# Gated mix of linear attention and a squared-ReLU network on one core: key sums through GpSimd, split piece transfers, low halves on VectorE, a fold by banks

## The chip, the core and the metric

The kernel runs on one core of a Trainium2 chip. Its time is the device time of one execution in microseconds (us); the kernel before the change takes 513.42 us (median of three runs, 512.58 to 514.22). A core has five engines, each with its own instruction queue that is worked off strictly in order: TensorE (PE, matrix products into the accumulation memory PSUM), VectorE (DVE), ScalarE (ACT), GpSimd (POOL) and SyncE (SP, which here only issues transfers). Transfers between memory and the on-chip SBUF, and inside SBUF, are issued by SP, ACT or GpSimd and carried by 16 DMA engines.

## The reference

```python
x = A_x                                     # 1 x 2048 x 512
g = sigmoid((x * gate_w).sum(-1))
qkv = x @ wqkv                              # 32 heads of 16
phi = lambda z: concat(softmax(z @ w_phi), softmax(-(z @ w_phi)))   # 32 features a head
kv  = einsum("sf,sd->fd", phi(k), v)        # per head
z   = phi(k).sum(over s)                    # per head: the key sums
o   = (phi(q) @ kv) / (phi(q) @ z + 1e-6)
a   = o @ wo
b   = relu(x @ w1 + b1) ** 2 @ w2 + b2      # 1792 hidden units
out = g * a + (1 - g) * b                   # everything in float32
```

## The kernel before

Every float32 product that matters is made of three faster ones: each operand is split into a high half (rounded, `hi`) and a low half (`src - hi`), and TensorE adds high x high, high x low and low x high (`mm3`, L76 to L78). ScalarE makes the high half, VectorE the low half (`split`, L61), except where the code names another engine.

The 2048 rows are worked in 4 blocks of 512, each block in 4 chunks of 128. There are two sweeps over the blocks. Sweep 1 runs the first 7 of the 14 hidden tiles of the network; between them it builds keys, values and the products phi(k)^T v, collected in the PSUM tile `kvps`. Sweep 2 runs the other 7 hidden tiles; between them it makes the queries, their features, numerators and the output projection. In both, `u` is the first network product (x times w1), `hh` and `hl` are the halves of its squared ReLU, `d` is the second (times w2). A table of slots (`at`) says after which `u` or `d` each other step is written; the order in which an engine then gets its instructions is made by a scheduler from that program, from priorities (`tc.high_priority`) and from pinned successions (`tc.issue_after`). So PE's order is: half a `u`, something of the attention, the other half, four chunks of `d`, and so on.

What happens between the sweeps and at the head of sweep 2, in the order of the work:

- `query_fold` (L192) multiplies w_phi into the query weights: 16 small matmuls on 32 x 32 corners of PE, row group r and column group g, bank r of four PSUM banks. ScalarE copies the banks out (`cp`), VectorE turns them, transfers lay them out (`wq`).
- `kv_most` and `kv_done` (L783, L791) bring `kvps` out in two parts. `kv_done` copies four groups of 17 rows (`kvt`), adds them to the first part on GpSimd (L796, four instructions), stores the key sums into `zrow` (L797) and spreads each half of `zrow` over all 128 partitions (L800, `vext`). Both kinds of transfer are issued by SP.
- For each query chunk n, `q_exps` (L362) takes maximum and minimum of the projected query tile `q`, subtracts, exponentiates on ScalarE (L343, tile `e`), and multiplies by the spread key sums on GpSimd (L368, `ez`, two instructions). `q_phi` (L371) reduces (`sm` L325, `dz` L378), works out the denominator in small steps (`r`, `dz`, `den`, `w`, L327 and L379 to L386) and scales `e` (L348).
- `transposed` (L392) turns 32 x 32 blocks on VectorE (`tb`, L394) and moves 12 pieces of 32 x 256 into `phiT` by transfers on SP's queue (L403); the four pieces on the diagonal are ScalarE copies (`diagonal`, L409).
- Two chunks make a pair. `numer` (L415) multiplies both chunks' `phiT` by the key-value blocks on PE (`num`, L420) and splits the result into `o`; ScalarE makes the high halves, VectorE the low ones. `attended` (L441) then multiplies `o` by the output weights (`att`). `phiT` and `o` have a single buffer, `tb` has two.

Two loads of x for the next block go by `do_x` (L627) and `load_x` (L110): in the block after the first of sweep 2 the low halves `xl` are GpSimd's, pinned behind the first `ez`; in the later blocks they are VectorE's.

Of the kernel before, what the change touches and what calls it, by code (L numbers as in the profile page):

```python
# [34 lines left out]
def tile_gated_mix(ctx: ExitStack, tc: tile.TileContext, xT, xn, wqT, wkT, wphi, wv, wo, w1, b1, w2, b2, gw, out):  # L35
# [25 lines left out]
    def split(src, hi, lo, ehi, elo):  # L61
        if ehi is nc.scalar:
            i = nc.scalar.activation(hi, src, AF.Copy)  # L63
        else:
            i = ehi.tensor_copy(hi, src)
        st["lo"] = elo.tensor_tensor(lo, src, hi.bitcast(F32), ALU.subtract)  # L66
        return i
# [39 lines left out]
        st["ffn"] = split(t, hi, lo, nc.scalar, nc.vector)  # L107
        return hi, lo

    def load_x(b, after=None):  # L110
        xs = []
        for k in range(NK):
            t = load(xT[b, :, k, :])
            hi = xpool.tile([P, SB], F32R, tag="xh", name=f"xh{b}_{k}")
            lo = xpool.tile([P, SB], F32R, tag="xl", name=f"xl{b}_{k}")
            with tc.issue_after(after.ins) if after else nullcontext():
                split(t, hi, lo, nc.scalar, nc.gpsimd if after else nc.vector)
            xs.append((hi, lo))
        return xs

# [71 lines left out]
    def query_fold():  # L192
        pss = [bank(f"fold{r}") for r in range(4)]
        wph, *t = st["wT"]
        for g in range(NK):
            for r in range(4):
                rows, cols = slice(32 * r, 32 * r + 32), slice(32 * g, 32 * g + 32)
                with tc.issue_after(st["up"].ins):
                    st["up"] = nc.tensor.matmul(
                        pss[r][cols, :], wph[rows, g * P + 32 * r:g * P + 32 * r + 32],  # L200
                        t[g][rows, :].rearrange("p (k c q) -> p c k q", c=4, q=32),
                        start=True, stop=True, skip_group_check=True)
        piece = lambda u, nm: work.tile([P, 2 * D], F32, tag=f"o{u}", name=nm, bufs=1)
        part_ = lambda t: t.rearrange("p (c k r q) -> p c k r q", c=2, k=NK, q=32)
        cps = [piece(u, "cp") for u in range(2)]
        for u, cp in enumerate(cps):
            for r in range(4):
                with tc.high_priority(offset=AHEAD):
                    nc.scalar.activation(
                        part_(cp)[:, :, :, r, :],  # L210
                        pss[r][:, 256 * u:256 * u + 256].rearrange("p (c k q) -> p c k q", c=2, q=32), AF.Copy)
        tbs = [work.tile([P, 2 * D], F32, tag="tb", name="turned", bufs=2) for _ in range(2)]
        for cp, tb in zip(cps, tbs):
            with tc.high_priority(offset=AHEAD):
                nc.vector.transpose(tb, cp)
        st["wq"] = [piece(u, "wq") for u in range(2)]
        for u, w in enumerate(st["wq"]):
            for c in range(4):
                for g in range(2):
                    (nc.sync, nc.gpsimd)[c % 2].dma_start(  # L220
                        w[32 * c:32 * c + 32, 512 * g:512 * g + 512],
                        tbs[c // 2][32 * (2 * u + g):32 * (2 * u + g) + 32, 512 * (c % 2):512 * (c % 2) + 512])
# [166 lines left out]

    def transposed(phi, pt, u):  # L392
        tb = work.tile([P, 2 * D], F32, tag="tb", name="tb", bufs=2)
        st["tb"] = nc.vector.transpose(tb, phi)  # L394
        later = []
        for j in range(4):
            for r in range(4):
                dst = pt[32 * j:32 * j + 32, u, r, :, :].rearrange("p g s -> p (g s)")
                src = tb[32 * r:32 * r + 32, 256 * j:256 * j + 256]
                if j == r:  # L400
                    later.append((dst, src))
                else:
                    st["pieces"] = nc.sync.dma_start(dst, src)  # L403
        return later

    def diagonal(n):
# [219 lines left out]

    def do_x(b):  # L627
        with tc.issue_after(st["act"].ins), tc.issue_after(st["pieces0" if b == NB + 2 else "act"].ins):
            st["x", b] = load_x(b % NB, st["ez"] if b == NB + 1 else None)

    ROWS = [divmod(o, 2) for o in (2, 3, 4, 5, 6, 7, 0, 1)]
    LASTP = len(ROWS) - 1
# [59 lines left out]
    def pair_steps(p, s):  # L692
# [19 lines left out]
        def run(i):  # L712
            first, other = i in (1, 2, 7), "Y" if i in (2, 7, 4) else "X"
            if i == 1:
                if p == 0:
                    banks.remove(ps_e)
                v["X"] = ps_e.tile([P, 512], F32, tag="s", name="pX")
            elif first:
                v["bank"] = banks[0]
                v["Y"] = bank("pY")  # L720
            elif i == 4:
                used(v["bank"])
            block(v[other], p, i, first)
            with tc.high_priority(offset=AHEAD), again(p, i, 0):
                if i in (1, 6, 5):
                    v[i] = st["tmp"][0][:, 512 * (i == 6):512 * (i == 6) + 512]
                    read = nc.scalar.activation(v[i], v["X"], AF.Copy)  # L727
                elif i == 7:
                    return
                else:  # L730
                    t, half, u = {2: (n, 0, 1), 3: (n, 1, None), 4: (m, 0, 6)}[i]
                    read = place(t, half, v[other], v.get(u))
            with tc.issue_after(read.ins):
                again(p, i, 1)
# [20 lines left out]
        if p == 0:  # L755
            at(s - 2, sums_add, p)
        at(s - 1.5 if p else s - 0.5, sums, p)
        for off, i in zip((0, 1, 1.5, 2, 2.5, 3, 4 - (p == LASTP) / 2), (1, 2, 6, 5, 7, 3, 4)):
            at(s + off, run, i)
        if p == LASTP:  # L760
            at(s + 3.5, banks.append, ps_e)
        at(s + 3, place7)
        at(s + 3, phi, n)
        at(s + 4, phi, m)
# [5 lines left out]
    def do_phi(b, n, c):  # L770
        with tc.high_priority(offset=AHEAD) if n < 2 else nullcontext():
            phi = q_phi(n)
            if c % 2 == 0:
                st["pt", n // 2] = work.tile([P, 2, 4, NG, 32], F32, tag="phiT", name="phiT", bufs=1)
            st["diag", n] = transposed(phi, st["pt", n // 2], c % 2)
        st.setdefault("pieces0" if n % 2 else "", st["pieces"])

    def do_n(pair):
# [12 lines left out]
    def kv_done():  # L791
        kvs = st["kvs"]
        for s in KV:
            with tc.high_priority(offset=AHEAD):
                nc.scalar.activation(st["kvt"][s, :], st["kv"][s, :], AF.Copy)
            nc.gpsimd.tensor_tensor(kvs[s, :], st["kvt"][s, :], kvs[s, :], ALU.add)  # L796
        nc.sync.dma_start(zrow.rearrange("(j x) -> j x", j=4), kvs[DH::32, :])  # L797
        for half in range(2):
            z = vext[2 * half][:, :D]
            nc.sync.dma_start(z, zrow[half * D:(half + 1) * D].partition_broadcast(P))  # L800
            zbc.append(z.rearrange("p (h f) -> p h f", f=DH))

    def kv_blocks():
# [195 lines left out]
```

## Time and profile before

| what | value |
|---|---|
| median of three runs | 513.42 us (512.58 to 514.22) |
| the profiled execution | 514.9 us, of which its span on the core is 513.1 us |
| mean granted PE clock over the span | 0.993 |
| busy share of the span: PE, DVE, ACT, POOL | 98%, 79%, 51%, 19% |
| the longest waits of PE | 2.7 us and 2.1 us, both on line L420 |

The profile is read from general to particular: busy shares, then what PE waited for, then the stretch where it waited, engine by engine in order of time. A row of a timeline gives start, duration, engine, line, operation, output from input, shape, number of merged instructions, and in brackets the idle time before it with what ended it. Starts of successive instructions on one engine may lie closer than the durations, since instructions overlap a little at their ends; what a step costs is best read from start to start.

### The profile page before, as it was taken

To read this page: it belongs to the slowest core of one execution; us is meant where nothing else is said; L and a number is where in the kernel's file an instruction comes from. 1 tells how busy PE (TensorE), PEld (TensorE's weight loads), DVE (VectorE), ACT (ScalarE), POOL (GpSimd) and SP (SyncE) were. 2 spreads that over 40 slices of the span, in tenths; PEclk is the share of its full clock that TensorE was granted. 3 is DMA by queue.
4 is the path that set the end of the run, shared out by engine and by line. 5 is a ranking of instruction groups with operands and counts; after the bars stand their busy time and mean duration, and the time that the engine had idled before them with its cause. 6 is when DMAs were issued, how large, how long until landed. Compare 5 with 4: busy or idle time off the path is not lost.

```text
span 513.1 us, 9416 instructions
## 1 busy us (share of the span) xinstructions
PE 502.5 (98%) x3520; PEld 403.8 (79%) x3520; DVE 405.6 (79%) x674; ACT 262.9 (51%) x482; POOL 98.2 (19%) x118
## 2 busy tenths in 40 slices
PE   9999999999999999999999969999999999999997
PEld 5878888878888888887888838878787878788775
DVE  5559967898695979788977879897969797897824
ACT  4887655465253475447782554354455344334540
POOL 1000141205400024000332622111112110111100
PEclk9999999999999999999999979999999999999999
DMA  8958687667854578771665131315212231032112
GB/s 264 280 184 279 201 298 236 193 216 233 284 190 160 176 237 299 246 232 29 167 191 219 32 112 40 105 33 169 58 31 83 70 86 42 10 107 79 37 28 82
DMA packets 46469, 77.18 MB, mean 150 GB/s; under 512 B 7124, under 2 KB 23256, under 8 KB 46424
## 3 DMA queue, kind: packets, MB, share of 16 engines
q1 hardware_dynamic: 36456, 42.30, 26.6%
q10 hardware_dynamic: 6768, 23.79, 13.8%
q0 software_dynamic: 3200, 10.49, 5.8%
q8 instruction: 28, 0.46, 0.4%
q14 instruction: 17, 0.14, 0.1%
HBM read 57.68 MB, written 11.54 MB: 135 GB/s over the span
## 4 chain that ended last, share of the span: by engine, by line
PE 80%; DMA 6%; DVE 6%; ACT 2%; SPq 2%; issue 2%; POOL 1%; DVEq 0%; POOLq 0%; ACTq 0%
PE d L76 8%; PE u L76 8%; PE d L77 8%; PE d L78 8%; PE u L77 8%; PE u L78 8%; PE pX L688 3%; PE att L78 3%; PE att L77 3%; PE att L76 3%; PE pX L690 3%; PE pX L689 3%; PE q L78 2%; PE q L77 2%; PE q L76 2%; DMA in<-in_xT 2%
## 5 line engine op out<-in xcount | busy, mean ns | idle before, releaser
L456 ACT ACTIVATE r<-u,b1c 128x512 f32<-128x512 f32 x56 | 38.4, 686 | 112.8 <-PE u L78 111.2
L76 PE MATMUL d<-w2h,hh 128*128 128x512 f32 x222 | 86.7, 391 | 0.0
L77 PE MATMUL d<-w2l,hh 128*128 128x512 f32 x222 | 86.4, 389 | 0.0
L78 PE MATMUL d<-w2h,hl 128*128 128x512 f32 x222 | 86.4, 389 | 0.0
L76 PE MATMUL u<-xh,w1h 128*128 128x512 f32 x212 | 83.8, 395 | 0.0
L77 PE MATMUL u<-xl,w1h 128*128 128x512 f32 x212 | 82.8, 391 | 0.0
L78 PE MATMUL u<-xh,w1l 128*128 128x512 f32 x212 | 82.6, 390 | 0.0
L368 POOL TENSOR_TENSOR ez<-e,vext 128x512 f32<-128x512 f32 x32 | 42.6, 1353 | 164.7 <-ACT e L343 158.6
L66 DVE TENSOR_TENSOR hl<-r,hh 128x512 fp32r<-128x512 f32 x56 | 38.9, 696 | 22.7 <-ACT hh L63 22.7
L76 PEld LDWEIGHTS d<-w2h,hh 128*128 128x128 f32 x222 | 41.7, 188 | 10.1 <-issue 1.4
L76 PEld LDWEIGHTS u<-xh,w1h 128*128 128x128 f32 x212 | 39.9, 188 | 11.7 <-issue 3.3
L78 PEld LDWEIGHTS d<-w2h,hl 128*128 128x128 f32 x222 | 41.7, 188 | 8.7
L77 PEld LDWEIGHTS d<-w2l,hh 128*128 128x128 f32 x222 | 41.7, 188 | 8.6
L78 PEld LDWEIGHTS u<-xh,w1l 128*128 128x128 f32 x212 | 39.9, 188 | 8.6 <-DVE w1l L66 0.2
L77 PEld LDWEIGHTS u<-xl,w1h 128*128 128x128 f32 x212 | 40.0, 189 | 8.0
L343 ACT ACTIVATE e<-e 128x1024 f32<-128x1024 f32 x27 | 28.6, 1060 | 33.3 <-DVE e L341 33.1
L325 DVE TENSOR_REDUCE sm<-e 128x64 f32<-128x1024 f32 x27 | 32.8, 1215 | 11.4 <-ACT e L343 11.4
L63 ACT ACTIVATE hh<-r 128x512 fp32r<-128x512 f32 x56 | 35.2, 628 | 1.1
L458 ACT ACTIVATE r<-r 128x512 f32<-128x512 f32 x56 | 34.9, 624 | 0.7
L409 ACT ACTIVATE phiT<-tb 32x256 f32<-32x256 f32 x64 | 26.4, 412 | 9.5 <-DVE tb L394 8.5
L378 DVE TENSOR_REDUCE dz<-ez 128x64 f32<-128x1024 f32 x16 | 19.4, 1215 | 14.9 <-POOL ez L368 14.9
L727 ACT ACTIVATE tmp<-pX 128x512 f32<-128x512 f32 x24 | 14.3, 598 | 29.7 <-PE pX L690 25.8
(188 smaller groups left out, 996.6 us busy)
## 6 DMA issues: line engine op xcount, KB each, us to landing
sloto<-wkeep ACTq DMA_DIRECT2D x30, 512.0 KB, 4.2
in<-in_xT SPq DMA_DIRECT2D x42, 256.0 KB, 4.5
slotez<-wkeep ACTq DMA_DIRECT2D x15, 512.0 KB, 5.7
phiT<-tb SPq DMA_DIRECT2D x192, 32.0 KB, 1.8
in<-in_w SPq DMA_DIRECT2D x23, 256.0 KB, 3.4
part<-row POOLq DMA_DIRECT2D x16, 256.0 KB, 5.6
row<-part SPq DMA_DIRECT2D x16, 256.0 KB, 3.1
out<-row SPq DMA_DIRECT2D x15, 256.0 KB, 2.2
```

The source lines that it names most:

```text
L63: i = nc.scalar.activation(hi, src, AF.Copy)
L66: st["lo"] = elo.tensor_tensor(lo, src, hi.bitcast(F32), ALU.subtract)
L76: nc.tensor.matmul(o, ah[:, sa], bh[:, sb], start=first, stop=False)
L77: nc.tensor.matmul(o, ah[:, sa], bl[:, sb], start=False, stop=False)
L78: return nc.tensor.matmul(o, al[:, sa], bh[:, sb], start=False, stop=last)
L325: nc.vector.tensor_reduce(sm, e3, AX.X, ALU.add)
L343: nc.scalar.activation(ef, ef, AF.Exp)
L368: st["ez"] = nc.gpsimd.tensor_tensor(ez[:, hs, :], e3[:, hs, :], zbc[half], ALU.mult)
L378: nc.vector.tensor_reduce(dz, ez, AX.X, ALU.add)
L409: nc.scalar.activation(dst, src, AF.Copy)
L456: st["relu"] = nc.scalar.activation(r, ps, AF.Relu, bias=b1c[:, fc:fc + 1])
L458: nc.scalar.activation(r, r, AF.Square)
```

## The change

Five things are changed, all around the head and the tail of sweep 2:

1. The key sums: the four additions of 17 rows become one of 128 rows, and the three transfers behind it (`zrow` out, and twice `vext` back) are issued by GpSimd, not SP.
2. For chunk 1 (the second of the first pair) and chunk 15 (the last of all), six of the twelve pieces go out by GpSimd's queue, the other six stay on SP's.
3. `load_x` makes all low halves on VectorE; the pin behind `ez` goes.
4. `query_fold` writes its matmuls bank by bank: for one r all four g, then the next r.
5. In the last key-value pair, the product of step 4 gets a doubled priority for its read-out, and `ps_e` returns to the list of banks before that step, not after.

```diff
@@ load_x
-    def load_x(b, after=None):
+    def load_x(b):
...
-            with tc.issue_after(after.ins) if after else nullcontext():
-                split(t, hi, lo, nc.scalar, nc.gpsimd if after else nc.vector)
+            split(t, hi, lo, nc.scalar, nc.vector)
@@ query_fold
-        for g in range(NK):
-            for r in range(4):
+        for r in range(4):
+            for g in range(NK):
@@ transposed
-    def transposed(phi, pt, u):
+    def transposed(n, phi, pt, u):
...
-                    st["pieces"] = nc.sync.dma_start(dst, src)
+                    queue = nc.gpsimd if n in (1, NB * NC - 1) and r % 2 else nc.sync
+                    st["pieces"] = queue.dma_start(dst, src)
@@ do_x
-            st["x", b] = load_x(b % NB, st["ez"] if b == NB + 1 else None)
+            st["x", b] = load_x(b % NB)
@@ pair_steps
-            with tc.high_priority(offset=AHEAD), again(p, i, 0):
+            with tc.high_priority(offset=2 * AHEAD if (p, i) == (LASTP, 4) else AHEAD), again(p, i, 0):
...
+        if p == LASTP:
+            at(s + 3.5, banks.append, ps_e)
         for off, i in zip((0, 1, 1.5, 2, 2.5, 3, 4 - (p == LASTP) / 2), (1, 2, 6, 5, 7, 3, 4)):
             at(s + off, run, i)
-        if p == LASTP:
-            at(s + 3.5, banks.append, ps_e)
@@ kv_done
-            nc.gpsimd.tensor_tensor(kvs[s, :], st["kvt"][s, :], kvs[s, :], ALU.add)
-        nc.sync.dma_start(zrow.rearrange("(j x) -> j x", j=4), kvs[DH::32, :])
+        nc.gpsimd.tensor_tensor(kvs, st["kvt"], kvs, ALU.add)
+        nc.gpsimd.dma_start(zrow.rearrange("(j x) -> j x", j=4), kvs[DH::32, :])
...
-            nc.sync.dma_start(z, zrow[half * D:(half + 1) * D].partition_broadcast(P))
+            nc.gpsimd.dma_start(z, zrow[half * D:(half + 1) * D].partition_broadcast(P))
```

Since the scheduler orders the program anew, instructions move on the engines beyond what the diff shows. The line numbers of the changed kernel are one lower from `query_fold` to `transposed`. Three places matter here.

GpSimd, from the key sums to the second chunk of the first pair. Before:

```order
L796 TENSOR_TENSOR vext_108<-vext_108 17x256 x4
L951 DMA part<-row 128x512 x4
L368 TENSOR_TENSOR ez<-e,vext_107 128x512
L368 TENSOR_TENSOR ez<-e,vext_109 128x512
L368 TENSOR_TENSOR ez<-e,vext_107 128x512
L368 TENSOR_TENSOR ez<-e,vext_109 128x512
L66 TENSOR_TENSOR xl_0_3344<-in,xh_0_3343 128x512
L66 TENSOR_TENSOR xl_1_3350<-in,xh_1_3349 128x512
L66 TENSOR_TENSOR xl_2_3356<-in,xh_2_3355 128x512
L66 TENSOR_TENSOR xl_3_3362<-in,xh_3_3361 128x512
```

The same stretch of GpSimd in the changed kernel:

```order
L796 TENSOR_TENSOR vext_108<-vext_108 128x256
L797 DMA zrow<-vext_108 4x256
L800 DMA vext_107<-zrow 128x512
L800 DMA vext_109<-zrow 128x512
L951 DMA part<-row 128x512 x4
L367 TENSOR_TENSOR ez<-e,vext_107 128x512
L367 TENSOR_TENSOR ez<-e,vext_109 128x512
L367 TENSOR_TENSOR ez<-e,vext_107 128x512
L367 TENSOR_TENSOR ez<-e,vext_109 128x512
L403 DMA phiT<-tb 32x256 x6
```

Three transfers now stand ahead of the stores of `part` and of the first `ez`; the four low halves are gone, and in their place stand six pieces of chunk 1.

VectorE, chunk 1 from its reduction `dz` to its transposition `tb`. Before:

```order
L378 TENSOR_REDUCE dz<-ez 128x64
L327 RECIPROCAL r<-sm 128x64
L66 TENSOR_TENSOR hl<-r,hh 128x512
L379 TENSOR_TENSOR dz<-dz,r 128x64
L382 SCALAR_TENSOR_TENSOR den<-dz 128x32
L383 RECIPROCAL den<-den 128x32
L384 TENSOR_SCALAR den<-den,gate 128x32
L386 TENSOR_TENSOR w<-r,den 128x64
L348 TENSOR_TENSOR e<-e,w 128x1024
L394 STREAM_TRANSPOSE tb<-e 128x1024
```

In the changed kernel, from the same `hl` on:

```order
L66 TENSOR_TENSOR hl<-r,hh 128x512
L378 TENSOR_TENSOR dz<-dz,r 128x64
L381 SCALAR_TENSOR_TENSOR den<-dz 128x32
L66 TENSOR_TENSOR xl_0_3341<-in,xh_0_3340 128x512
L382 RECIPROCAL den<-den 128x32
L66 TENSOR_TENSOR xl_1_3347<-in,xh_1_3346 128x512
L383 TENSOR_SCALAR den<-den,gate 128x32
L66 TENSOR_TENSOR xl_2_3353<-in,xh_2_3352 128x512
L385 TENSOR_TENSOR w<-r,den 128x64
L66 TENSOR_TENSOR xl_3_3359<-in,xh_3_3358 128x512
L347 TENSOR_TENSOR e<-e,w 128x1024
L393 STREAM_TRANSPOSE tb<-e 128x1024
```

The four low halves now lie between the small steps of chunk 1's denominator.

VectorE again, between the subtractions of chunk 3 and the low halves `o` of the first pair's numerators (the steps `dz`, `den`, `w`, `e`, `tb` here are chunk 2's). Before:

```order
L340 TENSOR_TENSOR e<-mn,q 128x32x16
L341 TENSOR_TENSOR e<-q,mx 128x32x16
L386 TENSOR_TENSOR w<-r,den 128x64
L348 TENSOR_TENSOR e<-e,w 128x1024
L66 TENSOR_TENSOR hl<-r,hh 128x512
L394 STREAM_TRANSPOSE tb<-e 128x1024
L66 TENSOR_TENSOR o<-num_3529,o 128x512
```

The changed kernel has there:

```order
L339 TENSOR_TENSOR e<-mn,q 128x32x16
L340 TENSOR_TENSOR e<-q,mx 128x32x16
L381 SCALAR_TENSOR_TENSOR den<-dz 128x32
L66 TENSOR_TENSOR hl<-r,hh 128x512
L382 RECIPROCAL den<-den 128x32
L383 TENSOR_SCALAR den<-den,gate 128x32
L385 TENSOR_TENSOR w<-r,den 128x64
L347 TENSOR_TENSOR e<-e,w 128x1024
L393 STREAM_TRANSPOSE tb<-e 128x1024
L66 TENSOR_TENSOR o<-num_3526,o 128x512
```

One `hl` and three small steps of chunk 2's denominator, which stood ahead of these subtractions, now stand behind them.

More of the change, by code (lines that the diff above doesn't have):

```diff
@@ L774, in do_phi @@
                 st["pt", n // 2] = work.tile([P, 2, 4, NG, 32], F32, tag="phiT", name="phiT", bufs=1)
-            st["diag", n] = transposed(phi, st["pt", n // 2], c % 2)
+            st["diag", n] = transposed(n, phi, st["pt", n // 2], c % 2)
         st.setdefault("pieces0" if n % 2 else "", st["pieces"])
```

## The prediction

> **What bounds the kernel now.** I read the busy shares first, then PE's waits, then PE's timeline where the longest of them lie.
>
> ```profile
> span 513.1 us, 9416 instructions
> PE 502.5 (98%) x3520; PEld 403.8 (79%) x3520; DVE 405.6 (79%) x674; ACT 262.9 (51%) x482; POOL 98.2 (19%) x118
> ...
> PE num L420 <- DMA phiT<-tb: 2.7, 1, 2.7
> PE num L420 <- ACT phiT L409: 2.1, 1, 2.1
> ```
>
> PE is busy for all but 10.6 us. Apart from head and tail it waits in one place of weight: the first pair's numerators, for the diagonal copies and then for the pieces of `phiT`. What that costs is seen beside the second pair, which does not wait (all rows PE):
>
> ```profile
> 297.33 0.39 PE L78 MATMUL u<-xh,w1l 128*128 128x512 f32 x1
> 299.83 1.03 PE L420 MATMUL num<-phiT,kvb 64*32 64x256 f32 x2 [2.11 <-ACT phiT L409]
> 303.51 1.96 PE L420 MATMUL num<-phiT,kvb 64*32 64x256 f32 x30 [2.65 <-DMA phiT<-tb]
> ...
> 307.40 0.39 PE L76 MATMUL d<-w2h,hh 128*128 128x512 f32 x1
> ...
> 311.94 0.39 PE L78 MATMUL att<-woh,o 128*128 128x512 f32 x1
> ...
> 333.02 0.39 PE L78 MATMUL u<-xh,w1l 128*128 128x512 f32 x1
> 333.34 1.09 PE L420 MATMUL num<-phiT,kvb 64*32 64x256 f32 x32
> ...
> 335.86 0.39 PE L76 MATMUL d<-w2h,hh 128*128 128x512 f32 x1
> ```
>
> From the last `u` before the numerators to the first `d` behind them the first pair takes 307.40 - 297.33 = 10.07 us, the second 335.86 - 333.02 = 2.84 us. So 7.23 us are lost. Idle time is 4.76 of that; the rest is a slower clock, as two stretches of 3.41 us show (PE busy time is the first number behind the comma, the granted clock the third number from the end):
>
> ```profile
> 296.28:299.69 3.41, 1.44 (x7) 0.86 (x5) 1.87 (x3) 2.60 (x5) 1.46 (x2) 1.00 0.21 57
> 299.69:303.10 3.41, 1.03 (x2) 0.18 (x2) 2.35 (x4) 1.75 (x3) 1.02 (x1) 0.50 0.18 48
> ```
>
> Everything behind `num` is PE without a gap, so 7.23 us is the most that this change can bring: 513.12 - 7.23 = 505.9 us of span.
>
> **Key sums by one addition and GpSimd's queue.** The chain of the first chunk, read from GpSimd's and ScalarE's timelines and from the transfers of `vext`:
>
> ```profile
> L795 ACT ACTIVATE vext<-kvps x4: 356/375/377, 254.9 to 256.1; 17x256 f32<-17x256 f32 x4
> 255.34 3.34 POOL L796 TENSOR_TENSOR vext<-vext 17x256 f32<-17x256 f32 x4 [7.37 <-ACT vext L795]
> L800 SPq DMA_DIRECT2D vext<-zrow x2: 320/363/406, 264.6 to 265.1; - x2
> DMA to landing us min/median/max: 6.7/7.1/7.4
> 268.51 1.05 ACT L343 ACTIVATE e<-e 128x1024 f32<-128x1024 f32 x1
> 271.63 2.54 POOL L368 TENSOR_TENSOR ez<-e,vext 128x512 f32<-128x512 f32 x2 [6.03 <-DMA in<-in_xT]
> ```
>
> The sums are ready at 258.68, but SP stores them only at 262.0 and spreads them at 264.6, and those transfers land about 7 us later; the page names another transfer as the releaser of 271.63, but 264.64 + 6.7 to 7.1 is that very moment. The exponentials were there at 269.56. Now the one addition starts when all four copies are in (256.1 + 0.4 = 256.5). It takes between one of the four (3.34 / 4 = 0.8) and an `ez` of twice its width (2.54 / 2 = 1.3): done by 257.8. In GpSimd's queue, at 0.6 us an issue and 2.9 us from issue to landing for a small transfer (row of `wq` below), `zrow` has landed by 260.7 and the second spread is issued from 261.3 on; at 7.4 us it lands at 268.7. Behind them wait the stores of `part` and `ez`; both are later anyway. So `ez` starts 0.14 us behind the exponentials (as at 298.23 below), at 269.70: **1.93 us earlier**, and chunk 1, which follows chunk 0 on VectorE, with it. If the spread were as late as before, this term is 0.
>
> **Low halves on VectorE.** Four instructions of about 0.6 us enter chunk 1's path, and GpSimd's four leave it:
>
> ```profile
> 274.21 1.22 DVE L378 TENSOR_REDUCE dz<-ez 128x64 f32<-128x1024 f32 x1 [3.40 <-POOL ez L368]
> 280.84 1.24 DVE L394 STREAM_TRANSPOSE tb<-e 128x1024 f32<-128x1024 f32 x1
> ...
> 286.11 5.49 POOL L66 TENSOR_TENSOR xl<-in,xh 128x512 fp32r<-128x512 f32 x4 [1.05 <-ACT xh L63]
> 285.09 1.22 DVE L378 TENSOR_REDUCE dz<-ez 128x64 f32<-128x1024 f32 x1 [1.32 <-POOL ez L368]
> 293.19 1.25 DVE L394 STREAM_TRANSPOSE tb<-e 128x1024 f32<-128x1024 f32 x1
> L379 DVE TENSOR_TENSOR dz<-dz,r x16: 209/215/1312, 276.3 to 480.9; 128x64 f32<-128x64 f32 x16
> ```
>
> While GpSimd works on `xl`, a VectorE step that takes 0.215 us elsewhere takes 1.31: in those 5.49 us each VectorE instruction with two SBUF operands waits for one of GpSimd's to end. So chunk 1 needs 8.10 us from `dz` to `tb`. Chunk 0, undisturbed and with five big instructions between its small ones, needs 6.63. The new chunk 1 also has five (one `hl`, four `xl`), so I take 6.63: `dz` at 285.09 - 1.93 = 283.16, `tb` at **289.79 instead of 293.19**. The other bound is 8.10 + 4 x 0.6 = 10.5, if the slow steps had another cause; then `tb` comes at 293.7.
>
> **Pieces by two queues.**
>
> ```profile
> 294.47 0.51 SPq L403
> ...
> 300.09 0.59 SPq L403
> ...
> L220 POOL DMA_DIRECT2D wq<-turned x8: 496/498/517, 243.9 to 247.5; - x8
> wq<-turned POOLq DMA_DIRECT2D x8, 64.0 KB, 2.9
> ```
>
> The first two rows are SP's first and tenth issue for chunk 1 in the chain of waits: 5.62 / 9 = 0.62 us apart. The twelfth starts at 294.47 + 11 x 0.62 = 301.3, and `num` runs 2.2 us later, at 303.51. With `tb` at 289.79 and done 1.25 us later, six on SP start from 291.05 to 294.2, and are usable at 296.4. GpSimd's six at 0.50 end at 294.05 and land by 296.5 (2.9 us from the last issue's start, for transfers twice as large). `num` is due at 297.65 (297.33 and the 0.32 of the second pair). **Both beat it: the wait of 4.76 us and its slow clock are gone.** The Trainium skill's page DMA: Bandwidth & Descriptors (section Latency and other measured facts) gives about 1 us to the first byte for transfers issued by GpSimd against 0.6 for SP; by that the pieces would be 0.4 us later on GpSimd than on SP (an estimate from that page), which changes nothing while 1.1 us are left. For chunk 15 the split is free: the last `num` did not wait.
>
> **What is late next.** `att` needs the low halves `o`, and VectorE makes them behind all of chunk 2. Its third matmul (L78, at 311.94) is the first to read them. Without the wait it is due at 311.94 - 7.23 = 304.71. When does VectorE get there?
>
> ```profile
> 296.25 0.68 DVE L341 TENSOR_TENSOR e<-q,mx 128x512 f32<-128x512 f32 x1
> 298.23 2.48 POOL L368 TENSOR_TENSOR ez<-e,vext 128x512 f32<-128x512 f32 x2 [6.63 <-ACT e L343]
> 305.51 0.69 DVE L341 TENSOR_TENSOR e<-q,mx 128x512 f32<-128x512 f32 x1
> 306.36 1.23 DVE L348 TENSOR_TENSOR e<-e,w 128x1024 f32<-128x1024 f32 x1
> 309.27 0.65 DVE L66 TENSOR_TENSOR o<-num,o 128x512 fp32r<-128x512 f32 x1
> 314.12 0.19 DVE L382 SCALAR_TENSOR_TENSOR den<-dz 128x32 f32<-128x32 f32 x1
> 315.27 1.23 DVE L348 TENSOR_TENSOR e<-e,w 128x1024 f32<-128x1024 f32 x1
> ```
>
> From `tb` to chunk 3's second subtraction it took 305.51 - 293.19 = 12.32. One `hl` (0.6) and three small steps (0.6 together, with overlap) have moved behind it, and the other `hl` fits where VectorE sat idle: 11.1, so 289.79 + 11.1 = 300.9. Behind it stand now the moved steps: 0.6 to the first of them, 1.15 from there to the product `e` (314.12 to 315.27), 0.6 for `hl`: `e` at 303.25. From `e` to `o` 2.91 less the `hl` that is gone, 2.3: `o` at 305.55, done at 306.2.
>
> But chunk 3's `ez` on GpSimd starts 1.98 us behind that subtraction (296.25 to 298.23), at 302.9, ahead of `e`, which reads two SBUF operands as the slow steps above do. By those rows it waits for one `ez` (1.24 us): `e` at 304.15, `o` done at 307.1; if also `w` just ahead of it is caught, each waits for one, and `o` is done at 308.5. In the old order `e` stood 0.85 us behind the subtraction and was through before `ez` came. PE then stands at `att` for 1.5, 2.4 or 3.8 us, and what is kept of 7.23 is **5.7, 4.8 or 3.4**. The order puts `ez` first by 0.3 us, so I take the two collided cases and their middle: **4.1 us**.
>
> Would that stall slow the clock too? The stretches above show the clock halved from 299.69 on, 1.97 us into an idle time (297.72 to 299.83); a stretch of 3.41 us of busy PE at half clock would cost 1.7 us.  I leave it out of the sum and put it in the range. The Trainium skill's page TensorE: Matmul & The Clock Gate (Part 1) asks for an idle window of about 3.4 us; by that a stall of 2.4 us costs no clock at all, where the row has it begin within 1.97.
>
> **Fold bank by bank.**
>
> ```profile
> L167 PE MATMUL fold<-row x128: 264/268/293, 26.7 to 29.0; 32*32 32x128 f32 x128
> L199 PE MATMUL fold<-row x32: 584/587/612, 236.9 to 238.3; 32*32 32x512 f32 x32
> 251.32 0.70 PE L357 MATMUL kvps<-e,vext 128*17 128x32 f32 x62
> ```
>
> 384 more columns take 0.319 us more, so a stream of 512 columns takes 0.425, and 32 streams 13.6 us one by one; they are done in about 2 because corners overlap. Now four successive products share a row group and differ in the column group. So do those of `kvps`, all of them: 62 streams of 32 columns would take 1.65 us one by one and take 0.70. So I take **0**, with up to 2 us if only four columns' worth overlap (13.6 / 4 = 3.4), which would largely vanish in the stall at `att`, since VectorE, not PE, sets that. What ScalarE gains by copying earlier it cannot use: VectorE works without a gap there. The swapped priority and `ps_e` move one VectorE instruction by 0.3 us, under matmuls that wait for nothing; I take 0, and 0.3 if that cover were gone.
>
> **Sum.** Span 513.12 - 4.1 = 509.0. The profiled execution was 514.9 with 1.8 around its span and lies 1.5 above the median; taken off the median, 513.42 - 4.1 = **509.3 us**.
>
> **The rivals.** *No collision*: `e` gets ahead of `ez`, or VectorE is quicker than I reckon; 513.42 - 5.7 = 507.7, at best 506.2. For it: the order is decided by 0.3 us. Against it: the exponentials and GpSimd have nothing else to wait for. Chance 0.28. *Less arrives*: the spread of the key sums lands as late as before, or the low halves cost VectorE their full time; 1.9 to 3.9 us of the chain are lost, or the stall at `att` halves the clock: 510.8 to 513.4. For it: GpSimd now stands in a wait for `zrow` with `part` and `ez` behind. Against it: 8 us lie between 261.3 and the end of the exponentials. Chance 0.17. *The fold runs one stream at a time*: it costs 13.6 - 2 = 11.6 us on PE, of which 7.2 fill the room that the wait leaves: 513.4 + 4.4 = 517.8; slower as soon as it costs more than 7.2. For it: all four row groups worked side by side before, and now one does. Against it: the `kvps` row. Chance 0.04. The Trainium skill's page TensorE: Matmul & The Clock Gate (Part 3, The mechanism) says that a weight load overlaps running matmuls only when the row group differs, which would bring exactly that; the `kvps` row, one row group throughout, disagrees.
>
> **How the numbers follow.** The likeliest case, 0.51, is 508.2 to 510.7. The range to hold it 8 times in 10 reaches into the first two rivals: 506.6 to 511.8. A change of under 0.3% (1.5 us) can't be told from none: faster than 511.9 are the likeliest case, the first rival and half of the second, 0.87; same 0.08; slower 0.05.
>
> **What would show it.** After the change: no wait of `num` on L420; `ez` of chunk 0 right behind its exponentials; `dz` of chunk 1 at 0.2 us; a new wait of PE at `att` for VectorE's `o` of 2.4 to 3.8 us, with an `e` on VectorE that takes above 2 us beside `ez`; `fold` in about 2 us. It is wrong if `num` still waits, if `att` doesn't, or if `fold` grows.

## The result, and the profile after

The changed kernel takes 511.23 us (median of 4 runs, 510.03 to 511.43); the kernel before, beside it on the same chip, 513.82 us (512.58 to 514.47). The ratio is 0.9948, with a 95% interval of 0.9922 to 0.9973. A second comparison gave 510.65 us against 514.44 us, ratio 0.9918 (0.9887 to 0.9949). So the change brings 0.5 to 0.8%; the medians differ by 2.6 and 3.8 us, where 4.1 us were forecast. The time lies in the range and 1.9 us above the forecast.

The profiled execution took 511.15 us with a span of 509.3 us. Its page and PE's waits (waited for: us in total, times, longest):

```profile
span 509.3 us, 9432 instructions
PE 501.8 (99%) x3520; PEld 404.1 (79%) x3520; DVE 405.6 (80%) x678; ACT 262.9 (52%) x482; POOL 99.5 (20%) x126
...
PE att L78 <- DVE o L66: 2.2, 1, 2.2
...
PE att L76 <- ACT r L456: 0.3, 1, 0.3
```

Both waits of `num` are gone, and a new one stands at `att`, for VectorE's `o`. PE's timeline, from `num` to the `q` behind `att`:

```profile
296.83 1.09 PE L420 MATMUL num<-phiT,kvb 64*32 64x256 f32 x32
...
303.91 0.50 PE L76 MATMUL att<-woh,o 128*128 128x512 f32 x1 [0.32 <-ACT r L456]
304.25 0.40 PE L77 MATMUL att<-wol,o 128*128 128x512 f32 x1
306.80 0.50 PE L78 MATMUL att<-woh,o 128*128 128x512 f32 x1 [2.16 <-DVE o L66]
...
307.70 0.63 PE L78 MATMUL att<-woh,o 128*128 128x512 f32 x1
308.13 0.63 PE L76 MATMUL att<-woh,o 128*128 128x512 f32 x1
...
310.69 0.49 PE L76 MATMUL q<-wqh,xh 128*128 128x512 f32 x1
```

Behind the wait the matmuls start 0.43 us apart rather than 0.23: half clock. The windows of that stretch (PE's busy time is the first number behind the comma, the granted clock the third from the end) show where:

```profile
300.65:304.06 3.41, 3.09 (x14) 2.24 (x14) 3.31 (x7) 2.61 (x4) 1.60 (x2) 1.00 0.00 0
304.06:307.47 3.41, 1.25 (x5) 0.72 (x6) 3.38 (x5) 1.24 (x3) 1.96 (x1) 1.00 0.00 0
307.47:310.89 3.42, 3.42 (x10) 2.64 (x9) 3.39 (x5) 1.56 (x4) 0.00 (x0) 0.50 0.22 58
```

A stretch of 3.41 us with 1.25 us of work in it is followed by one at half clock. The sum closes: the twelve `att` matmuls, due from 303.59 (303.91 less 0.32) and 0.227 us apart, would have ended with `q` at 306.3; `q` starts at 310.69, so 4.4 us are lost, and 7.23 - 4.4 = 2.8 are kept. Measured from the first `d` behind the query fold to the end of the span, the kernel before takes 274.27 us and the changed one 271.53: 2.7 us less. The spans differ by 3.8 us; 0.8 of the rest comes from the fold itself (below), and 0.3 had arisen ahead of it.

Why `o` is late, and the chain that leads there, on GpSimd and VectorE:

```profile
256.26 0.74 POOL L796 TENSOR_TENSOR vext<-vext 128x256 f32<-128x256 f32 x1 [8.57 <-ACT vext L795]
...
269.27 2.55 POOL L367 TENSOR_TENSOR ez<-e,vext 128x512 f32<-128x512 f32 x2 [3.94 <-ACT e L342]
...
302.45 3.56 POOL L367 TENSOR_TENSOR ez<-e,vext 128x512 f32<-128x512 f32 x2 [5.48 <-ACT e L342]
```

```profile
282.74 1.22 DVE L377 TENSOR_REDUCE dz<-ez 128x64 f32<-128x1024 f32 x1 [1.32 <-POOL ez L367]
...
284.88 0.21 DVE L378 TENSOR_TENSOR dz<-dz,r 128x64 f32<-128x64 f32 x1
...
289.38 1.25 DVE L393 STREAM_TRANSPOSE tb<-e 128x1024 f32<-128x1024 f32 x1
...
300.47 0.68 DVE L340 TENSOR_TENSOR e<-q,mx 128x512 f32<-128x512 f32 x1
...
302.43 0.23 DVE L385 TENSOR_TENSOR w<-r,den 128x64 f32<-128x64 f32 x1
302.69 2.20 DVE L347 TENSOR_TENSOR e<-e,w 128x1024 f32<-128x1024 f32 x1
304.92 1.25 DVE L393 STREAM_TRANSPOSE tb<-e 128x1024 f32<-128x1024 f32 x1
306.09 1.25 DVE L66 TENSOR_TENSOR o<-num,o 128x512 fp32r<-128x512 f32 x2
```

The first chunk's `ez` now waits for nothing but its exponentials, chunk 1's small steps are quick again (0.21 us), `tb` comes at 289.38. Then chunk 3's `ez` starts 0.24 us ahead of chunk 2's product `e`, which takes 2.20 us where it takes 1.22 alone. The small step `w` started 0.02 us ahead of that `ez` and was not caught.

### The profile page after: what moved, and what is told of

The parts are those of the page before. It is cut to its first block, busy times and chain, and to the rows that moved or that the text cites. A ratio compares the mean times of both kernels' runs of the same rounds, so it can differ in the third digit from the quotient of the medians.

```text
span 509.3 us, 9432 instructions
## 1 busy us (share of the span) xinstructions
PE 501.8 (99%) x3520; PEld 404.1 (79%) x3520; DVE 405.6 (80%) x678; ACT 262.9 (52%) x482; POOL 99.5 (20%) x126
## 4 chain that ended last, share of the span: by engine, by line
PE 81%; DVE 8%; ACT 4%; DMA 3%; POOL 1%; issue 1%; SPq 0%; ACTq 0%; POOLq 0%; DVEq 0%
PE d L76 8%; PE d L77 8%; PE d L78 8%; PE u L76 8%; PE u L77 7%; PE u L78 7%; PE att L78 3%; PE pX L688 3%; PE att L77 3%; PE att L76 3%; PE pX L690 3%; PE pX L689 3%; PE q L76 2%; PE q L78 2%; PE q L77 2%; PE pY L689 2%
```

## The experiments

Twelve kernels were run in three groups, each group (1 to 4, 5 to 8, 9 to 12) beside its own runs of the kernel before, whose medians were 514.44, 514.12 and 514.61 us. The third column counts from the first `d` behind the query fold to the end of the span of the profiled execution, which leaves out what differs at the head; the fourth counts the stretches of 3.41 us at half clock in which PE still had work.

| kernel | median (runs), us | ratio to before (95%) | behind the fold, us | half clock |
|---|---|---|---|---|
| before, first comparison | 513.82 (4) | 1 | 274.3 | 2 |
| changed, first comparison | 511.23 (4) | 0.9948 (0.9922 to 0.9973) | 271.5 | 1 |
| 1 changed, again | 510.65 (6) | 0.9918 (0.9887 to 0.9949) | 272.8 | 2 |
| 2 `o` first | 510.01 (6) | 0.9906 (0.9879 to 0.9933) | 271.5 | 1 |
| 3 chunk 3's exponentials later | 507.50 (5) | 0.9865 (0.9845 to 0.9885) | 269.1 | 0 |
| 4 old fold order | 509.83 (6) | 0.9919 (0.9896 to 0.9943) | 272.0 | 1 |
| 5 `o` between | 505.92 (4) | 0.9842 (0.9824 to 0.9860) | 267.8 | 0 |
| 6 pieces on one queue | 509.07 (4) | 0.9914 (0.9882 to 0.9946) | 270.4 | 0 |
| 7 key sums undone | 512.85 (10) | 0.9978 (0.9964 to 0.9993) | 274.7 | 2 |
| 8 low halves undone | 509.54 (4) | 0.9913 (0.9894 to 0.9931) | 270.9 | 0 |
| 9 key sums alone | 512.28 (9) | 0.9951 (0.9933 to 0.9969) | 272.4 | 1 |
| 10 as 5, one queue | 509.95 (4) | 0.9920 (0.9891 to 0.9949) | 271.5 | 1 |
| 11 as 5, low halves undone | 508.57 (4) | 0.9889 (0.9864 to 0.9914) | 269.6 | 0 |
| 12 one addition, SP's queue | 510.61 (4) | 0.9932 (0.9908 to 0.9956) | 272.0 | 1 |

### 1. The changed kernel again

No edit.

> The changed kernel once more, beside the three kernels below on one chip. If the 2.6 us between the medians are the whole of the gain, the ratio to the kernel before stays at 0.995; if the 3.8 us between the two profiled spans are, it comes to 0.9926. Either way PE should stand for about 2.2 us at the third matmul of att and run at half clock for one stretch of 3.41 us behind it.

The ratio is 0.9918, nearer to the larger gain. The wait at `att` is 2.15 us again, but the half clock lasted two stretches, not one:

```profile
301.86:305.27 3.41, 1.66 (x7) 0.73 (x5) 3.37 (x3) 1.18 (x3) 3.33 (x2) 1.00 0.00 0
305.27:308.69 3.42, 2.71 (x6) 2.15 (x7) 3.42 (x6) 2.80 (x6) 0.00 (x0) 0.50 0.13 36
308.69:312.10 3.41, 3.41 (x9) 2.64 (x8) 3.20 (x9) 0.00 (x0) 0.00 (x0) 0.50 0.19 51
```

The same wait fell otherwise on the grid of stretches: 0.7 us of it lay in the first halved one. The six times reach from 507.89 to 512.74, and the mean granted clocks go with them: 1.000 and 0.999 for the two fastest (507.89 and 508.99 us), 0.996 for 509.81 us, 0.993 for the three slowest (511.49 to 512.74). One stretch of 3.41 us at half clock takes about 0.003 off the mean of a span of 510 us, so by these means the same kernel runs with two such stretches, with one, and with none.

### 2 and 3. Taking the wait at `att` away

Kernel 2 writes chunk 2's features behind the first numerators and pins chunk 2's `dz` behind `o`:

```diff
-        with tc.issue_after(st["num"].ins) if n % 2 and n > 1 else nullcontext():
+        with tc.issue_after(st["num"].ins) if n % 2 and n > 1 or n == 2 else nullcontext():
             nc.vector.tensor_reduce(dz, ez, AX.X, ALU.add)
...
-        at(s, do_phi, NB + q, n, n % NC)
+        at(s + 4 * (p == 1), do_phi, NB + q, n, n % NC)
```

> The changed kernel with chunk 2's features written behind the first pair's numerators, and chunk 2's dz pinned behind the low halves o; on VectorE o then stands right behind chunk 3's subtractions and nothing of chunk 2's features stands ahead of it. Theory (what is missing of the 7.23 us is the stall at att and the half clock that follows it): by the durations of the changed kernel's timeline the subtractions end at 298, the exponentials at 299.2, the high halves at 300.2 and the low halves at 301.0, so att, due at 304.6, does not wait for o; the stall of 2.16 us and the 1.7 us of half clock go, about 3.9 us: 507.3 us. Rival 1 (a stall at att costs its own length only, the clock slows for another reason): 2.2 us less, 509.0 us, with a stretch at half clock still there. Rival 2 (chunk 2 and 3 come too late for the second pair): a wait of that pair's num takes back 1 to 4 us, 509 to 511 us.

Kernel 3 only lets chunk 3's maxima, minima and subtractions stand behind chunk 2's reciprocal, so that `e` gets ahead of `ez`:

```diff
-        with tc.issue_after(st["den" if n == 1 else "tb"].ins) if n in (1, 2) else nullcontext():
+        with tc.issue_after(st["den" if n != 2 else "tb"].ins) if n in (1, 2, 3) else nullcontext():
             e3, r = exps(ps, late=n == 3)
```

> The changed kernel with the maxima, minima and subtractions of chunk 3 pinned behind chunk 2's reciprocal of den. VectorE does the same work up to o, but e times w now stands one hl and one w behind the last subtraction, ahead of chunk 3's ez, as it did in the kernel before. Theory (e took 2.20 us rather than 1.22 because it waited for GpSimd's ez): e takes 1.22 us, o ends 1.0 to 1.1 us earlier and att waits 1.1 us rather than 2.16. If a wait that short leaves the clock whole, 1.1 + 1.7 = 2.8 us less: 508.4 us; if the clock halves all the same, 510.1 us. Rival (e is slow for another reason, or att waits for something else): e still above 2 us, att still waits 2 us, 511.2 us.

Kernel 2 has no wait at `att`, and yet 510.01 us: its rival 2 came true. Chunks 2 and 3 are late, and the second pair's `num` waits 2.49 us for its pieces, with half a clock behind it:

```profile
327.15 1.09 PE L420 MATMUL num<-phiT,kvb 64*32 64x256 f32 x30 [2.49 <-DMA phiT<-tb]
```

Kernel 3 is the test of the collision. Its VectorE does the same instructions, and `e` takes 1.22 us; GpSimd's `ez` comes later, runs into `e`, and is the one that waits (2.95 us rather than 2.54):

```profile
299.33 0.68 DVE L340 TENSOR_TENSOR e<-q,mx 128x512 f32<-128x512 f32 x1
...
300.67 1.22 DVE L347 TENSOR_TENSOR e<-e,w 128x1024 f32<-128x1024 f32 x1
```

```profile
301.31 2.95 POOL L367 TENSOR_TENSOR ez<-e,vext 128x512 f32<-128x512 f32 x2 [6.36 <-ACT e L342]
```

`att` waits 0.98 us for ScalarE and 0.29 for `o`, and the clock stays whole. Counted from chunk 2's `dz`, `o` comes 1.0 us sooner, as expected. Behind the fold that is 269.1 us, 2.4 less than in the changed kernel where 2.8 were expected; that the time, 507.50 us, is still under the expected 508.4 would then come from ahead of the fold, where its profiled execution is 1.95 us quicker than that of the changed kernel. The ratios 0.9865 and 0.9918 of one group have intervals that do not meet: collision and half clock were what the changed kernel left lying.

### 4. The fold's order

```diff
-        for r in range(4):
-            for g in range(NK):
+        for g in range(NK):
+            for r in range(4):
```

> The changed kernel with the old order of the fold (for each g all r). Its last stream of 32 matmuls should take 2.02 us again rather than 1.24. Theory (the 0.78 us that the fold gained are swallowed, since att waits for VectorE): PE comes to att 0.78 us later and waits 1.4 us rather than 2.16; same time within 0.4 us, 511.2 us, or 509.5 us if the shorter wait leaves the clock whole. Rival (the fold's gain reaches the end): 0.8 us more, 512.0 us.

The time is that of the changed kernel, but neither reason was tested: the old order is as fast as the new, and `att` waits 2.14 us for `o` as before (and 0.78 us rather than 0.32 for ScalarE ahead of that). PE's timeline at the fold, for the kernel before:

```profile
236.90 2.02 PE L199 MATMUL fold<-row 32*32 32x512 f32 x32
```

For the changed kernel:

```profile
236.65 1.24 PE L198 MATMUL fold<-row 32*32 32x512 f32 x32
```

For kernel 4, with the old order in the changed kernel:

```profile
235.14 1.22 PE L198 MATMUL fold<-row 32*32 32x512 f32 x32
```

And for kernel 9 below, which is the kernel before with the new key sums:

```profile
236.39 2.05 PE L199 MATMUL fold<-row 32*32 32x512 f32 x32
```

So the 0.8 us belong to what kernel 4 has and kernel 9 has not. Low halves and split are not it: without the one or the other (kernels 8 and 6) the fold takes 1.27 and 1.28 us. That leaves the doubled priority and the bank list. In the kernel before, the fold's third product writes into the bank of `pY`, and the program has it wait for VectorE's last reading of it, ahead of which stands an `hl`. VectorE's timeline of the kernel before, and PE's weight loads:

```profile
236.34 0.69 DVE L66 TENSOR_TENSOR hl<-r,hh 128x512 fp32r<-128x512 f32 x1
236.95 0.41 DVE L709 TENSOR_TENSOR vext<-tmp,pY 128x256 f32<-128x256 f32 x1
```

```profile
236.90 0.14 PEld L199 LDWEIGHTS fold<-row 32*32 32x32 f32 x4 [0.35 <-issue]
237.48 0.17 PEld L199 LDWEIGHTS fold<-row 32*32 32x32 f32 x4 [0.44 <-issue]
```

The reading ends at 237.36, and the loads go on at 237.48, 0.12 us later; in kernel 9 they go on 0.12 us behind the same reading too. So the view's "issue" is most likely this wait. In the changed kernel VectorE reads ahead of the `hl`, and is through at 236.48, before the fold starts at 236.65 (in kernel 4 it is through at 234.97, ahead of 235.14):

```profile
236.07 0.41 DVE L709 TENSOR_TENSOR vext<-tmp,pY 128x256 f32<-128x256 f32 x1
236.40 0.68 DVE L66 TENSOR_TENSOR hl<-r,hh 128x512 fp32r<-128x512 f32 x1
```

Neither the priority nor the bank list was run alone; these traces and the program's waits speak for the priority, and that is argued, not shown.

### 5. `o` between: no wait left to speak of

Kernel 5 lets chunk 3's subtractions fill VectorE's idle 1.5 us ahead of chunk 2's `dz`, and puts `o` between chunk 2's small steps and its `e`. It moves `do_phi` as kernel 2 does, and:

```diff
-            nc.vector.tensor_tensor(e[:, :, 0, :], pv, bc(mx), ALU.subtract)
+            st["sub"] = nc.vector.tensor_tensor(e[:, :, 0, :], pv, bc(mx), ALU.subtract)
...
-        with tc.issue_after(st["num"].ins) if n % 2 and n > 1 else nullcontext():
+        with tc.issue_after(st["num" if n % 2 else "sub"].ins) if n > 1 and n < 3 or n % 2 and n > 1 else nullcontext():
             nc.vector.tensor_reduce(dz, ez, AX.X, ALU.add)
...
-        return scaled(e3, w.rearrange("p h t -> p (h t)"))
+        with tc.issue_after(st["num"].ins) if n == 2 else nullcontext():
+            return scaled(e3, w.rearrange("p h t -> p (h t)"))
```

> The changed kernel with chunk 2's features written behind the first pair's numerators, chunk 2's dz pinned behind chunk 3's last subtraction, and chunk 2's scaled e pinned behind the low halves o. So VectorE makes chunk 3's subtractions while it used to sit idle for 1.5 us, then chunk 2's small steps, then o, then e and tb of chunk 2. Against the kernel with the late exponentials of chunk 3, which still had 0.98 us (for ScalarE) and 0.29 us (for o) of waits at att and 269.1 us from the first d behind the query fold to the end. Theory (every microsecond of wait at att is a microsecond of time, and e and tb of chunk 2 are not urgent): no wait at att, whole clock, 267.9 us behind the fold, 506.2 us in all. Rival (as in the kernel with o first, chunk 2 comes too late for the second pair's num): a wait of 1 to 2.5 us there, 507.5 to 509 us.

505.92 us, 0.9842 of the kernel before (0.9824 to 0.9860): this beats both kernels, and its four times lie within 0.25 us (505.81 to 506.06). One wait of 0.63 us is left at `att`, for the collision has moved to two small steps on VectorE, beside an `ez` that runs on GpSimd from 298.66 to 301.52:

```profile
299.03 1.31 DVE L378 TENSOR_TENSOR dz<-dz,r 128x64 f32<-128x64 f32 x1
300.38 1.19 DVE L381 SCALAR_TENSOR_TENSOR den<-dz 128x32 f32<-128x32 f32 x1
```

### 6 to 8. One part of the change undone at a time

Kernel 6 sends all pieces by SP (`queue = nc.sync`):

> The changed kernel with all twelve pieces of chunks 1 and 15 on SP's queue again; the order on every other engine is the same. The twelve are then usable 0.62 x 11 + 2.2 = 9.0 us behind the first issue at 290.6, at 299.6, where num is due at 296.8: a wait of 2.8 us. Theory (without the split att waits less by what num waits more, since VectorE's o is ready at the same time; the parts of the change overlap): att's third matmul is due at 307.4 rather than 304.6 and o is there at 306.7, so the end moves by 0.6 us: 511.5 to 512 us, up to 1.7 more or less by the clock. Rival (the split is worth its own wait): 2.8 us more, 514 us.

Kernel 7 has the four additions and SP's three transfers of the key sums again:

> The changed kernel with the key sums as before: four additions of 17 rows, and zrow and its two spreads by SP's queue. The order on VectorE, ScalarE and PE is the same as in the changed kernel. Theory (the chain from the key sums to o sets the end): chunk 0's ez starts 2.0 to 2.4 us later, so do tb and o; num waits about 1.9 us, att's third matmul starts 2.0 to 2.4 us later: 513 to 514 us, with one more stretch of half clock up to 1.7 more. Rival (the low halves and the split alone bring the gain): less than 0.5 us more, 511 to 511.7 us.

Kernel 8 has `load_x` and `do_x` of the kernel before:

> The changed kernel with the low halves of the next x on GpSimd again, pinned behind ez as before. VectorE's order goes back to that of the kernel before, in which e of chunk 2 stands ahead of the late ez. Theory (GpSimd's low halves slow chunk 1's small steps on VectorE): dz to tb takes 8.1 us rather than 6.6, and the small step dz 1.3 us rather than 0.2; tb comes at 290.8, num waits about 0.9 us, o is done by the old distances at 307.5 rather than 306.7: 0.8 us more, 512 us, up to 1.7 more by the clock; e takes 1.2 us. Rival (the slow steps have another cause, and VectorE only gains work by the change): dz to tb takes 4.2 us, 510 us or less.

Kernel 6: PE waits at `num` instead of at `att`, and the time is no longer than with two queues. The row of PE's waits:

```profile
PE num L420 <- DMA phiT<-tb: 2.1, 1, 2.1
```

Behind the fold it takes 270.4 us; the changed kernel without its half clock would take 271.5 - 1.7 = 269.8, so the 0.6 expected are there. But the wait lay across two stretches, which kept 2.63 and 2.13 us of work, and the clock was not halved in this execution; the 509.07 us are 2.4 under the forecast's lower end, of which 1.7 had been allowed for the clock. Kernel 8 reads alike: `dz` to `tb` takes 289.80 - 281.71 = 8.09 us again, `e` 1.22 us, PE waits 0.41, 0.73, 1.00 and 0.28 us in four places, and the clock stays whole. Its 270.9 us are 1.1 above those 269.8, where 0.8 were expected, but its time, 509.54 us, is not the 512 forecast. The small step beside GpSimd's `xl`:

```profile
284.49 1.31 DVE L379 TENSOR_TENSOR dz<-dz,r 128x64 f32<-128x64 f32 x1
```

Neither part brings anything measurable in this kernel: by these traces, the half clock behind the late `o` takes back what each saves. Kernel 7 has 0.9978, 1.5 us more than the changed kernel by the first comparison and 3.1 by the second; behind the fold it is 1.9 us slower than run 1, which also has two halved stretches. That is the lateness of its chain: counted from the first `d` behind the fold, chunk 0's `ez` starts 1.97 us later than in the changed kernel and `o` 1.89 us later, though `num` waits 0.61 us rather than the 1.9 expected and `att` 0.97 and 2.13.

### 9. The key sums alone

The kernel before, with the `kv_done` part of the diff and nothing else.

> The kernel before with the key sums of the change alone (one addition, zrow and its spreads by GpSimd's queue). The order on VectorE, ScalarE and PE is that of the kernel before, fold order included. Theory (the earlier key sums carry the gain; low halves and split bring nothing here, as their two undone kernels had the time of the changed one): the chain from ez to o comes 1.9 to 2.4 us earlier, num still waits, about 2.7 us rather than 4.76, o is there when att comes, and dz still takes 1.3 us in chunk 1: 2.0 us from waits and 0 to 1.7 us from one stretch less of half clock, 510.3 to 512 us on the scale of 514. Rival (the parts need each other): 513 us or more. The fold, in its old order, should take 1.2 us if the 2.02 us of the first profile were that execution's own, 2.0 if the order makes it slow.

512.28 us against 514.61, ratio 0.9951: 2.5 us. `num` waits 2.90 us rather than 4.76, and one stretch runs at half clock rather than two. All the rest without the key sums (kernel 7) brings 0.9978, 1.1 us, 0.8 of which is the fold. Together that is 3.6 us, between the two measurements of the whole.

### 10 and 11. The same parts undone where nothing else is late

> The kernel of 505.9 us (o before chunk 2's e) with all pieces on SP's queue; every other engine's order is the same. Theory (what the split is worth depends on what waits behind num): num waits 2.1 us and starts 2.6 us late in all as in the changed kernel with one queue, but nothing at att is late any more: 0.6 us of wait go, 2.0 us more, 507.9 us. Rival (the split is worth nothing here either): 506 us.

> The kernel of 505.9 us with the next x's low halves on GpSimd again. Theory (the low halves on VectorE take 1.45 us out of chunk 1's chain, and now nothing gives it back): dz to tb takes 8.1 us rather than 6.6, num waits about 1 us, o comes at about 303.5 rather than 302.4: 1.1 us more, 507 us. Rival (VectorE's four added instructions cost as much as the undisturbed small steps gain): 506 us.

By the ratios, in kernel 5 the split is worth 4.0 us (0.9920 against 0.9842): `num` waits 2.16 us without it, and this time the wait fell into one stretch and halved the next. Without that, 271.5 - 1.7 - 267.8 = 2.0, as expected. The low halves are worth 2.4 us (0.9889) and 1.8 behind the fold, where 1.1 were expected: `num` waits 0.45 us for ScalarE and `att` 1.32 for `o`. Both parts do what they were reckoned to do, once nothing else takes their place.

### 12. One addition, or GpSimd's queue?

Kernel 12 keeps the one addition and gives the three transfers back to SP.

> The changed kernel with the one addition of the key sums kept, but zrow and its spreads by SP's queue. Theory (the queue makes the difference, since SP stands in front of zrow with loads of wo and the weights until 261 or 262 in either case): chunk 0's ez starts where it does with both undone, 1.9 us later than in the changed kernel: 512.5 to 513 us. Rival (the three additions less bring it): ez as early as in the changed kernel, 510.5 to 511.3 us.

The theory fell: 510.61 us, as the changed kernel, and the first `ez` starts right behind its exponentials with SP's queue as well. GpSimd's timeline in kernel 12:

```profile
268.55 1.29 POOL L367 TENSOR_TENSOR ez<-e,vext 128x512 f32<-128x512 f32 x1 [3.94 <-ACT e L342]
270.10 1.30 POOL L367 TENSOR_TENSOR ez<-e,vext 128x512 f32<-128x512 f32 x1 [0.27 <-DMA vext<-zrow]
```

SP's loads of `wo` are not on a clock of their own. VectorE's turn of the key-value tile waits for the sums, the low halves `wol` stand behind it, the next load of `wo` stands behind them on its buffer, and `zrow` behind that load. In kernel 7 the four copies of the sums start at 253.15; VectorE's and SP's timelines behind them:

```profile
256.94 0.45 DVE L805 STREAM_TRANSPOSE vext<-vext 128x256 f32<-128x256 f32 x1 [3.05 <-POOL vext L796]
```

```profile
257.99 1.70 SPq L272 DMA_DIRECT2D in<-in_wo  x4
...
260.25 0.59 SPq L797 DMA_DIRECT2D zrow<-vext  x1
```

In kernel 12 the copies start at 253.93:

```profile
256.29 0.45 DVE L805 STREAM_TRANSPOSE vext<-vext 128x256 f32<-128x256 f32 x1 [1.61 <-POOL vext L796]
```

```profile
257.34 1.90 SPq L272 DMA_DIRECT2D in<-in_wo  x4
...
259.80 0.60 SPq L797 DMA_DIRECT2D zrow<-vext  x1
```

Counted from the copies, all three come 1.4, 1.4 and 1.2 us earlier with one addition. The links between them are read from the order and the equal shifts; none was cut by itself. GpSimd's queue adds what is left: in kernel 12 the second `ez` still waits 0.27 us for its transfer. The other half of the question, four additions with GpSimd's queue, was not run.

## Why the prediction came out as it did

**The bound.** 505.9 us of span was given as the most the change could bring; kernel 5, with 504.1 us, goes below it by 1.8. Behind the fold the bound is 274.3 - 7.2 = 267.1, and kernel 5 takes 267.8; what the bound left out lies ahead, 2.5 us: the fold's wait (0.8) and 1.7 by which executions differ at the head.

**Key sums.** `ez` was put 0.14 us behind the exponentials at 269.70; it starts at 269.27, 0.09 us behind them, and undoing the part (kernel 7) makes it 1.97 us later where 1.93 were reckoned. Right. But SP's queue was taken for the reason of the old delay, and kernel 12 shows that one addition is enough with SP's queue too; whether GpSimd's queue would be enough with four stays open.

**Low halves.** `dz` to `tb` 6.63 us, measured 6.64; `tb` at 289.79, measured 289.38. Right, with the mechanism: the kernel before and kernels 8, 9 and 11 show 1.3 us for chunk 1's small step beside GpSimd's `xl`, all others 0.21.

**Two queues.** No wait at `num`. Right; undoing it brings 2.07 us of wait back (kernel 6). The 0.4 us by which the pieces were to come later on GpSimd's queue than on SP's do not show: from issue to landing the median is 1.8 us on both.

**What is late next.** Right in place and size: `att` at its third matmul, 2.16 us where the case of one `ez` had 2.4, `e` at 2.20 us. The two waits at `att`, 2.16 and 0.32 us, would by themselves have kept 4.75 of 7.23. The sum, though, was the middle of two cases, 4.8 and 3.4, and the second, in which `w` is caught too, was missed by 0.02 us. The rival in which `e` gets ahead was built as kernel 3 and has 507.50 us beside 514.44, 6.9 us less; forecast were 507.7 beside 513.42, 5.7 less.

**The clock.** Here the step failed: "I leave it out of the sum and put it in the range". The wait does halve the clock in both traces of the changed kernel, for one stretch of 3.41 us (1.7 us) or two, and in eight of its ten executions the mean granted clock is 0.996 or lower. What stands on record as a condition of the rival *less arrives* belonged into the likeliest case: 513.42 - 4.1 + 1.7 = 511.0, and 511.23 was measured (the 510.8 on record for that rival is 0.2 lower than its own terms give). That the two lie so close is partly luck: with the case that came true, 4.8 kept, the same sum gives 510.3, and one kernel's times differ by more than that. The sentence on the Trainium skill's page TensorE: Matmul & The Clock Gate (Part 1), that a stall of 2.4 us would cost no clock, was the wrong half of that weighing. The row that had it begin within 1.97 us was nearer, but no rule by itself: 2.07 us of wait that lay across two stretches halved none in the trace of kernel 6.

**Fold and priority.** The order's 0 is right (kernel 4). "The swapped priority and `ps_e` move one VectorE instruction by 0.3 us, under matmuls that wait for nothing" is wrong: most likely the fold's third product waited for it, 0.8 us that the profile listed as time of the fold. The 2.02 us of that row were taken as the fold's own. The bound of up to 2 us more for the order does not follow from its own sum either: 3.4 - 2.0 is 1.4.

## What to carry to other kernels

Price a part of a change by what is late once it is gone: split and low halves brought nothing measurable here, and 4.0 and 2.4 us in kernel 5, because in the changed kernel one late `o` and the half clock behind it took their place. The length of a wait on PE is not its price: the traces of kernel 6 and of run 1, each with a wait of 2.1 to 2.2 us, took 2.6 and 5.0 us longer behind the fold than kernel 5, in good part by where the wait fell in the clock's stretches. So splitting or shortening a wait can gain more than its length. And a group of matmuls that is slower than its shape explains may hide a wait for a bank's last reader, so its weight loads are worth a look.

## What the runs showed of the hardware

**The clock goes by stretches of 3.41 us that run on by themselves.** In the changed kernel, run 1, kernel 2 and kernel 7 a stretch with 1.25, 1.66, 1.31 and 1.73 us of PE work was followed by one at half clock; with the grid counted on from the start of the clock's record, full-clock stretches with 2.13 (kernel 6) and more were not:

```profile
296.96:300.37 3.41, 2.13 (x35) 1.50 (x36) 3.41 (x9) 0.38 (x1) 0.00 (x0) 1.00 0.58 160
300.37:303.79 3.42, 3.42 (x17) 2.83 (x16) 3.28 (x6) 2.24 (x4) 2.59 (x2) 1.00 0.45 164
```

So among the stretches inside the span the bound lies between half and five eighths of a stretch. The last products at the end of the span do not fit that: stretches with 1.42 us (kernel 9) and 1.46 us (kernel 12) were followed by half clock there, but one with 1.74 us (kernel 6, from 501.75) and one with 1.59 us (the kernel before, from 507.90) were not. So about half a stretch of work is where it turns, and PE's busy time, whose ends are modelled, gives no sharper bound. A halved stretch with 2.71 us of work was followed by another halved one (run 1); one with 3.00 us, in the kernel before, was not. The Trainium skill's page TensorE: Matmul & The Clock Gate (Part 1) gives a free-running window of 3413 ns; the traces agree. It lets the clock fall after an idle window; here a window up to half at work was enough.

This makes one kernel's times spread. With a wait of 2.15 us they reach over 4.9 us (run 1); with 0.63 us, over 0.25 (kernel 5). It is not all of the spread: kernel 3's times differ by 1.6 us at a mean clock of 1.000 throughout. Where the first `d` behind the fold starts also differs between executions, from 235.9 to 238.9 us over these traces; beyond the fold's 0.8 us that was not explained.

**VectorE and GpSimd hold each other up both ways.** The later of two overlapping instructions with two SBUF operands waits: `e` 2.20 us beside an earlier `ez`, `ez` 2.95 us beside an earlier `e`. The Trainium skill's page SBUF — State Buffer (section SBUF: two separate sides) has the two engines share a port pair as an exclusive lock, taken by whichever starts first; both rows agree. It holds for small steps too: 1.31 us rather than 0.21 for 64 columns.
